# Projection tiles ahead of an attention loop as two 64-row halves side by side

## The chip, the cores and the metric

The kernel runs on one core of a Trainium2 chip. The metric is device time in microseconds (us) of one execution, as the median of several runs. Engines are named as in the profile: PE (TensorE; PEld is its weight load), DVE (VectorE), ACT (ScalarE), POOL (GpSimd), and SP, whose queue issues nearly all DMAs.

## The reference

The input x is 1 x 2048 x 512. After a layer norm without weights, xn goes through attention with 32 heads of 16, and through an MLP that gates the attention's output:

```python
qkv = (xn @ wqkv).reshape(B, S, 3, 32, 16)          # -> q, k, v
p = softmax(einsum("bhqd,bhkd->bhqk", q, k) * 16**-0.5)
s = einsum("bhqk,bhkd->bhqd", p, v) -> (B, S, 512) @ wo
h = relu(xn @ w1 + b1) ** 2                         # 512 -> 1792
g = silu(h @ w2 + b2)                               # 1792 -> 512
out = x + s * g
```

## The kernel before

**Numbers.** All matmuls are fp32r. A product is made from high and low parts of both factors, hi*hi + hi*lo + lo*hi (`terms3`), so a 128 x 512 tile of a projection with a contraction of 512 takes 4 x 3 = 12 matmuls of 128 x 128 by 128 x 512.

**Stages.** First comes the layer norm, with PE transposes and the first projection tiles. Then, ahead of the main loop, 48 rounds of score maxima (`for rnd in range(2 * LEAD)`, L1186). Then the loop of 512 slots, each of which makes exponentials of one block of keys for four heads, P times V, maxima for a later unit, and a share of the MLP. In the loop a slot already runs 64-row matmuls in two lanes: rows 0 to 63 and rows 64 to 127 of the array work on different things at the same time, in different banks.

**A round.** `max_mm(g, j)` for j = 0, 1 (L298 and L305) makes one 64-row matmul of q by k in lane j into a PSUM bank, and DVE reduces the bank to its maxima. Lane 0 uses a bank of pool `pe` (named se, three banks), lane 1 one of pool `pm` (pm_t, three banks). Every third round calls `pump(24)`, which issues 24 matmuls of the projections still to be made: two tiles, one in the bank of pool `pd` (pd_t), one in that of `pv` (po), with all 128 rows (L972 for q and k, L1019 for v). Some rounds also issue loads (`max_end`), the making of a unit's shift (`shift`, L333: four small DVE operations, a store to sh_d and four loads of qe rows from it; here at round 36), the split of the second half of wr_t (round 7) and two splits of w1 (`split_w1`, on POOL, rounds 37 and 41).

**Evacuation of a tile.** A v tile is copied by ACT into a vt buffer and stored (L1025, L1028). A q or k tile is copied by ACT into `raw` (two buffers, L996); POOL makes the high part (L83) and the low part (L84) in `hl` (three buffers); SP stores both parts (L927, `qk_store`). The tiles with m = 0 are split from PSUM by ACT and DVE (`split_psum`, L89 and L90). The last tile, `qk_tile(7, 3, True)`, is left to the first two slots of the loop, which pump six of its matmuls each (L1208), into pd_t.

**Order.** In this stage PE, ACT, DVE and POOL take their instructions in the order of the program. SP's order isn't written out: a planner of the framework lays it from its own estimates, and in the loop SP follows the program too. Every engine works through its queue in order.

Of the kernel before, what the change touches and what calls it, by code (L numbers as in the profile page):

```python
# [9 lines left out]
F32 = mybir.dt.float32  # L10
F32R = mybir.dt.float32r
AF = mybir.ActivationFunctionType
# [5 lines left out]
P = 128  # L18
# [3 lines left out]
DH = 16  # L22
F = 1792
KO = D // P
# [9 lines left out]
NVT = 7  # L34
# [7 lines left out]
def kernel(  # L42
# [11 lines left out]
    nc = tc.nc  # L54
# [24 lines left out]
    def split(dst, raw, hi_act=False, lo=None):  # L79
        if hi_act:  # L80
            nc.scalar.activation(dst[0], raw, AF.Copy)
        else:
            nc.gpsimd.tensor_scalar(dst[0], raw, 1.0, 0.0, op0=ALU.mult, op1=ALU.add)  # L83
        (lo or nc.gpsimd).tensor_tensor(  # L84
            dst[1], raw, dst[0].bitcast(F32), op=ALU.subtract
        )

    def split_psum(hi, lo, ps):
        nc.scalar.activation(hi, ps, AF.Copy)  # L89
        nc.vector.tensor_tensor(lo, ps, hi.bitcast(F32), op=ALU.subtract)  # L90
# [8 lines left out]
    with ExitStack() as ph:  # L99
# [823 lines left out]
        def qk_store(m, c, hl):  # L923
            cs = slice(c * 512, (c + 1) * 512)
            dst = q_d[m] if m < 4 else k_d[m - 4]
            for i in range(2):
                nc.sync.dma_start(dst[i, :, cs], hl[:, i].bitcast(F32))  # L927
# [21 lines left out]
        def when_done(fn):  # L949
            if hold[0]:  # L950
                held.append(fn)
            else:
                fn()

        def let_go():
            while held:
                held.pop(0)()
# [9 lines left out]
        def qk_tile(m, c, last=False):  # L967
            ps = pd.tile([P, 512], F32, name="pd_t") if last else qkv_bank()

            for n0, n1 in ((0, 256), (256, 512)) if c == 0 and m % 4 == 0 else ((0, 512),):  # L970
                for out_, lh, rh, first_, last_ in qk_terms(m, c, ps):
                    nc.tensor.matmul(  # L972
                        out_[:, n0:n1], lh(slice(0, P)), rh(slice(0, P))[:, n0:n1],
                        start=first_, stop=last_,
                    )
                    if not last_ or n1 < 512:
                        yield
            if last:

                hl = pools["n"].tile([P, 2, 512], F32R, name="hl")  # L980
                raw = sp.tile([P, 512], F32, name="ot", bufs=1)
                nc.scalar.activation(raw, ps, AF.Copy)
                split((hl[:, 0], hl[:, 1]), raw)
                later(6, lambda: qk_store(m, c, hl))
                yield
                return

            quick = m % 4 == 0 and not hold[0]

            def evac():  # L990
                hl = hlp.tile([P, 2, 512], F32R, name="hl")
                if quick:
                    split_psum(hl[:, 0], hl[:, 1], ps)
                else:
                    raw = hlp.tile([P, 512], F32, name="raw", bufs=2)
                    nc.scalar.activation(raw, ps, AF.Copy)  # L996
                    split((hl[:, 0], hl[:, 1]), raw)
                qk_store(m, c, hl)

            when_done(evac)  # L1000
            yield

        def qk_first():
            tiles = [qk_tile(m, 0) for m in (4, 0)]
# [3 lines left out]
                        next(tile_)  # L1008
                        yield

        def v_tile(c, tt):
            xT = xTs[c]
            ps = qkv_bank()
            ts_ = slice(tt * P, (tt + 1) * P)
            for out_, lh, rh, first_, last_ in terms3(ps, [
                (lambda a, q, ko=ko: xT[q, a, ko, ts_], lambda b, q, ko=ko: wa_t[q, b, ko, 2 * P :])
                for ko in range(KO)
            ]):
                nc.tensor.matmul(out_, lh(slice(0, P)), rh(slice(0, P)), start=first_, stop=last_)  # L1019
                if not last_:  # L1020
                    yield

            def evac():
                vt = vts[(4 * c + tt) % NVT]
                nc.scalar.activation(  # L1025
                    vt[:, :, :DH], ps.rearrange("p (h d) -> p h d", d=DH), AF.Copy
                )
                nc.sync.dma_start(v_d[:, c * 4 + tt, :], vt.rearrange("p h d -> p (h d)"))  # L1028

            when_done(evac)  # L1030
            yield

        xts = {}

# [41 lines left out]

        ahead = []
        rest = []

        def pump(n):  # L1080
            for _ in range(n):
# [30 lines left out]
        for i in range(NT + 3):  # L1112
            if i in (2, 3):

                kos = slice(2 * i - 4, 2 * i - 2)
                if i == 2:
                    ln_norm(1)
                    ln_high(0)
                    split_w(wa_t, kos, slice(0, 2 * P), raw_m[:, kos])
                else:  # L1120
                    ln_low(0)
                    ln_high(1)
                    split_w(wa_t, kos, slice(0, 2 * P), raw_m[:, kos])
                    ln_norm(2)
                ln_stats(i)
            else:
                if i < NT:
                    ln_stats(i)
                if 0 <= i - 1 < NT:
                    ln_norm(i - 1)  # L1130
                if 0 <= i - 3 < NT:
                    ln_low(i - 3)
                if i == 4:

                    pump(4)
                if 0 <= i - 2 < NT:
                    ln_high(i - 2)
            if 5 <= i < 9:
                split_w(wa_t, i - 5, slice(2 * P, 2 * P + D), raw_v[:, i - 5], True)
            let_go()  # L1140
            if 9 <= i < 11:
                fill_ring("ka", 1, 1.0, (32 + 64 * (i - 9),))
            if i in (11, 12):
                fill_ring("qm", i - 11, 0.0)
            if i == 11:
                raw_r = [load_w("wv", 3 * P, ((P, 3 * P),))]
            if i >= 4:
                pump({4: 4, 7: 14, 8: 12}.get(i, 8 if i < 7 else 7))
            if i == 3:
                ahead.append(qk_first())  # L1150
            if i >= 7 and (i - 3) % 4 == 3:
                c = (i - 3) // 4
                ahead.append(qk_tile(4, c))
                rest.append(qk_tile(0, c))
            if i >= 3 and (i - 3) % 4 == 3:
                c = (i - 3) // 4
                rest += [v_tile(c, tt) for tt in range(4)]
        let_go()
        hold[0] = False
        while ahead:  # L1160
# [12 lines left out]
            fill_ring("qe", n, 0.0)  # L1173
        for n in (2, 3):
            fill_ring("ka", n, 1.0)
        rest += [
            qk_tile(m, c, (m, c) == (7, 3)) for c in range(4) for m in (1, 5, 2, 6, 3, 7)
        ]

        pump(47)  # L1180
        led.append(0)
        pump(24)
        warm = const.tile([P, 1], F32, name="warm")
        nc.scalar.activation(warm, eps_t, AF.Exp)

        for rnd in range(2 * LEAD):  # L1186
            g = rnd // 2
            if rnd % 2 == 0:
                shift_due(g)
            for j in range(2):  # L1190
                max_mm(g, j, None if j else lambda: pe.tile([P, 512], F32, name="se"))
            if rnd % 3 == 2:
                pump(24)
            if rnd % 2 == 0:
                continue
            max_end(g)
            if g == 0:
                raw_r = [load_w("wv", 3 * P, ((D + P, 3 * P),))]
            if g == 3:
                for ko in range(KO):  # L1200
                    split_w(wr_t, ko, slice(3 * P, 6 * P), raw_r[0][:, ko])
                ln.close()
                pools["v"] = ph.enter_context(tc.tile_pool(name="vp", bufs=1))
            if g == 12:
                s1.close()
                ep = ph.enter_context(tc.tile_pool(name="ep", bufs=1))
                rot["pt"] = [ep.tile([P, 512], F32, name=f"pt{i}") for i in range(NPT)]
                pools["n"] = ph.enter_context(tc.tile_pool(name="np", bufs=1))  # L1208
                mlp_early()
            if g in (18, 20):  # L1210
                split_w1((g - 18) // 2)
                load_w1(3 + (g - 18) // 2)
            if g == 16:
                for fo in range(3):
                    load_w1(fo)
                load_v(0)
                nc.sync.dma_start(b1_t, b1.rearrange("(fo p) -> p fo", p=P), allow_slow_non_contiguous=True)
                nc.sync.dma_start(b2_t, b2[None, :].to_broadcast([P, D]))
            if g % 2 and g < 16:
                c, i = divmod(g // 2, 2)  # L1220
                nc.sync.dma_start(
                    xn_d[i, :, :, c * 512 : (c + 1) * 512], xTs[c][:, i].bitcast(F32)
                )
        first.close()

        def exp_mm(st, j, pts, spare):
# [175 lines left out]
        done = 0  # L1402
# [61 lines left out]
```

## Time and profile before

| | |
|---|---|
| median of three runs | 1638.34 us (1637.03 to 1639.03) |
| span of the profiled execution, first to last instruction | 1635.6 us |
| mean granted TensorE clock of it | 0.999 |
| busy: PE, DVE, ACT, POOL | 99%, 83%, 73%, 32% |

The profile is of one execution, and its span leaves out what lies before the first and after the last instruction; the runs' times hold it. A row of the timeline gives start and length in us, engine, line, operation, output and inputs, and in brackets the idle time of the engine before it with what ended it. `64*128 64x512` is a matmul on 64 rows of the array, `128*128 128x512` one on all rows. Matmuls overlap, so their pitch is read from their starts.

### The profile page before, as it was taken

How to read it: one execution, taken by the hardware profiler on the slowest of the kernel's cores; microseconds unless marked ns; L12 is line 12 of the kernel's file. 1: busy time of each engine (PE TensorE's matmuls, PEld its weight loads, DVE VectorE, ACT ScalarE, POOL GpSimd, SP SyncE). 2: the span in 40 equal slices, each digit the busy share in tenths (PEclk: the TensorE clock that was granted, in tenths of full speed). 3: DMA queues.
4: the chain of work that ended last, by engine and by line, in shares of the span. 5: the costliest groups of instructions: out<-in, count | busy, mean ns of one | idle time of the engine just before them, and what ended most of it. 6: DMA issues, size and time to landing. Idle time of an engine off the chain costs nothing.

```text
span 1635.6 us, 35352 instructions
## 1 busy us (share of the span) xinstructions
PE 1620.8 (99%) x13300; PEld 923.2 (56%) x13300; DVE 1356.8 (83%) x2345; ACT 1189.9 (73%) x2351; POOL 523.0 (32%) x547
## 2 busy tenths in 40 slices
PE   8999999999999999999999999999999999999998
PEld 6777565456546655664466456645654565445543
DVE  6356888888888888888888888888888888887754
ACT  7311777777777777877777777777777777777786
POOL 6446568123112311321133112311321233125421
PEclk9999999999999999999999999999999999999999
DMA  8768655434333333434343334323532353246654
GB/s 299 193 210 276 205 171 145 125 100 124 83 95 100 109 93 81 129 87 112 79 121 89 83 90 141 101 68 88 147 98 61 88 144 81 60 130 195 193 170 155
DMA packets 164418, 209.18 MB, mean 128 GB/s; under 512 B 59928, under 2 KB 78872, under 8 KB 162712
## 3 DMA queue, kind: packets, MB, share of 16 engines
q1 hardware_dynamic: 163960, 206.40, 44.5%
q8 instruction: 105, 1.72, 0.5%
q14 instruction: 65, 0.53, 0.1%
q10 hardware_dynamic: 288, 0.52, 0.1%
HBM read 149.95 MB, written 56.61 MB: 126 GB/s over the span
## 4 chain that ended last, share of the span: by engine, by line
PE 99%; DVE 1%; DMA 0%; issue 0%; ACT 0%; POOL 0%; DVEq 0%; POOLq 0%
PE po L373 31%; PE pd_t L242 18%; PE pm_t L298 18%; PE se L1234 15%; PE pd_t L210 6%; PE pd_t L972 2%; PE po L972 2%; PE se L1019 1%; PE se L972 1%; PE pd_t L1019 1%; PE se L298 1%; PE po L1019 1%; PE pm_t L1234 1%; PE pm_t L1065 0%; PE pm_t L811 0%; DVE mx L305 0%
## 5 line engine op out<-in xcount | busy, mean ns | idle before, releaser
L305 DVE TENSOR_REDUCE mx<-pm_t 128x1 f32<-128x512 f32 x2000 | 1245.1, 684 | 167.8 <-PE pm_t L298 77.3
L1246 ACT ACTIVATE pt<-se 128x512 f32<-128x512 f32 x2002 | 1044.2, 617 | 257.6 <-PE se L1234 214.5
L298 PE MATMUL pm_t<-ka,qm 64*128 64x512 f32 x2000 | 793.7, 420 | 1.5 <-DVE mx L305 1.3
L1234 PE MATMUL se<-qe,ka 64*128 64x512 f32 x2002 | 674.0, 396 | 0.2 <-ACT pt L1246 0.2
L373 PE MATMUL po<-pt,v 128*32 128x512 f32 x4096 | 545.3, 604 | 0.0
L298 PEld LDWEIGHTS pm_t<-ka,qm 64*128 64x128 f32 x2000 | 350.1, 184 | 244.8 <-DVE mx L305 230.7
L242 PEld LDWEIGHTS pd_t<-xc,w1s 64*128 64x128 f32 x2688 | 334.0, 187 | 93.9 <-issue 88.9
L242 PE MATMUL pd_t<-xc,w1s 64*128 64x256 f32 x2688 | 380.2, 288 | 0.0
L1234 PEld LDWEIGHTS se<-qe,ka 64*128 64x128 f32 x2002 | 337.6, 184 | 20.7 <-ACT pt L1246 2.6
L242 PE MATMUL pd_t<-w2t,hT 64*128 64x512 f32 x1080 | 300.6, 410 | 0.0
L242 PEld LDWEIGHTS pd_t<-w2t,hT 64*128 64x128 f32 x1080 | 179.1, 184 | 80.5 <-issue 75.5
L529 POOL TENSOR_TENSOR r<-r 128x512 f32<-128x512 f32 x56 | 58.2, 1040 | 374.9 <-ACT r L526 374.9
L373 PEld LDWEIGHTS po<-pt,v 128*32 128x32 f32 x4096 | 81.0, 108 | 158.8 <-issue 136.4
L548 POOL TENSOR_TENSOR u<-u,b_t 128x512 f32<-128x512 f32 x16 | 20.6, 1287 | 316.3 <-ACT u L547 316.3
L411 POOL TENSOR_TENSOR ot<-ot,hl 128x512 f32<-128x512 f32 x31 | 39.8, 1284 | 204.4 <-DMA hl<-r_d 91.1
L210 PE MATMUL pd_t<-wot,oc 64*128 64x512 f32 x336 | 90.9, 406 | 0.0
L526 ACT ACTIVATE r<-pd_t,b_t 128x256 f32<-128x256 f32 x112 | 46.9, 470 | 57.1 <-PE pd_t L242 57.1
L210 PEld LDWEIGHTS pd_t<-wot,oc 64*128 64x128 f32 x336 | 58.4, 184 | 45.4 <-ACT pt L1246 14.2
L84 POOL TENSOR_TENSOR hT<-r,hT 128x512 fp32r<-128x512 f32 x56 | 72.2, 1290 | 4.7
L210 PE MATMUL pd_t<-w2t,hT 64*128 64x512 f32 x264 | 68.8, 393 | 0.0
L305 DVE TENSOR_REDUCE mx<-se 128x1 f32<-128x512 f32 x48 | 32.9, 685 | 40.0 <-PE pm_t L298 30.0
L210 PEld LDWEIGHTS pd_t<-w2t,hT 64*128 64x128 f32 x264 | 47.0, 184 | 6.0
(129 smaller groups left out, 928.5 us busy)
## 6 DMA issues: line engine op xcount, KB each, us to landing
w1s<-w_d SPq DMA_DIRECT2D x196, 256.0 KB
qm<-q_d SPq DMA_DIRECT2D x384, 32.0 KB
ka<-k_d SPq DMA_DIRECT2D x96, 128.0 KB
qe<-q_d SPq DMA_DIRECT2D x384, 32.0 KB
xn_d<-xT SPq DMA_DIRECT2D x8, 1024.0 KB
k_d<-hl SPq DMA_DIRECT2D x32, 256.0 KB
q_d<-hl SPq DMA_DIRECT2D x32, 256.0 KB
xc<-xn_d SPq DMA_DIRECT2D x16, 512.0 KB
```

Of the source, the lines that this page charges most:

```text
L84: (lo or nc.gpsimd).tensor_tensor(dst[1], raw, dst[0].bitcast(F32), op=ALU.subtract)
L210: mm = nc.tensor.matmul(out_, lh(r), rh(r), start=first_ and lane == 0, stop=last_ and lane == 1, skip_group_check=True,)
L242: mm = nc.tensor.matmul(out_, lh(r), rh(r), start=first_ and lane == 0, stop=last_ and lane == 1, skip_group_check=True,)
L298: nc.tensor.matmul(ps, qms[u][p][64 * j : 64 * j + 64, qb * P : (qb + 1) * P], kas[qd, p][64 * j : 64 * j + 64, kc * 512 : (kc + 1) * 512] ...
L305: return nc.vector.tensor_reduce(mxs[u][:, c, kc : kc + 1], ps, axis=AX.X, op=ALU.max)
L373: nc.tensor.matmul(po[32 * j : 32 * j + 32, :], vs[qd][:, (4 * kb + j) * VW : (4 * kb + j) * VW + 32], pts[j], start=(kb == 0), stop=(kb = ...
L526: nc.scalar.activation(r[:, i], ps[:, i * CW : (i + 1) * CW], AF.Relu, bias=b1_t[:, fo : fo + 1])
L529: nc.gpsimd.tensor_tensor(r, r, r, op=ALU.mult)
L972: nc.tensor.matmul(out_[:, n0:n1], lh(slice(0, P)), rh(slice(0, P))[:, n0:n1], start=first_, stop=last_,)
L1019: nc.tensor.matmul(out_, lh(slice(0, P)), rh(slice(0, P)), start=first_, stop=last_)
L1234: nc.tensor.matmul(se, kas[qd, j // 2][b : b + 64, kb * P : (kb + 1) * P], qes[u][j // 2][b : b + 64, :], start=True, stop=True,)
L1246: return nc.scalar.activation(pts[j], se, AF.Exp, scale=0.25)
```

## The change

The 32 tiles that the rounds make are issued by a generator, `side_rounds`, which takes them in groups of four: two in banks of `pm`, two in those of `pd` and `pv`. Each of the 12 matmuls of a tile becomes two of 64 rows. A group has four parts of 12 steps, and a step is one half matmul of one tile in lane 0 and one of another tile in lane 1: tiles 0 and 1; then 2 and 3; then 1 and 0, the lanes crossed; then 3 and 2. After the third part tiles 1 and 0 are evacuated, after the fourth 3 and 2. Every round issues eight steps, so a group takes six rounds and there are eight groups. Both maxima of a round now use banks of `pe`. At the start of a crossed part each lane's first matmul waits, by an added dependency, for the other lane's maximum of a round in between (`since`), so that the two lanes don't write one bank at the same time. The evacuation is moved into functions `qk_done` and `v_done`; tile (m, c) = (0, 3) is now evacuated over `raw` as the others. Ahead of the rounds, the pump stops at the end of tile (0, 2). `qk_tile(7, 3, True)` is left to the slots as before.

```diff
+        def side_tile(kind, a, b, ps):
+
+            if kind == "v":
+                return v_terms(a, b, ps), lambda: v_done(a, b, ps)
+            return qk_terms(a, b, ps), lambda: qk_done(a, b, ps, False)
+
+        def side_rounds(specs):
+
+            assert len(specs) % 4 == 0
+            for n in range(0, len(specs), 4):
+                banks = [pm.tile([P, 512], F32, name="pm_t") for _ in range(2)]
+                tiles = [side_tile(*spec, ps) for spec, ps in zip(specs[n : n + 2], banks)]
+                for part, (a, b) in enumerate(((0, 1), (2, 3), (1, 0), (3, 2))):
+                    if part == 1:
+                        banks = [pd.tile([P, 512], F32, name="pd_t"), pv.tile([P, 512], F32, name="po")]
+                        tiles += [
+                            side_tile(*spec, ps) for spec, ps in zip(specs[n + 2 : n + 4], banks)
+                        ]
+                    for k in range(3 * KO):
+                        for lane, tile_ in enumerate((a, b)):
+                            r = slice(64 * lane, 64 * lane + 64)
+                            out_, lh, rh, first_, last_ = tiles[tile_][0][k]
+                            mm = nc.tensor.matmul(
+                                out_, lh(r), rh(r),
+                                start=first_ and part < 2, stop=last_ and part > 1,
+                                skip_group_check=True,
+                            )
+                            if k == 0 and part > 1:
+                                tc.add_manual_dep(
+                                    mm.ins, since[part][1 - lane].ins.name,
...
+                        yield part, k
+                    if part > 1:
+                        for tile_ in (a, b):
+                            tiles[tile_][1]()
...
-        rest += [
-            qk_tile(m, c, (m, c) == (7, 3)) for c in range(4) for m in (1, 5, 2, 6, 3, 7)
+        rest += [qk_tile(7, 3, True)]
+        later_tiles += [
+            ("qk", m, c) for c in range(4) for m in (1, 5, 2, 6, 3, 7) if (m, c) != (7, 3)
         ]
 
         pump(47)
         led.append(0)
-        pump(24)
+        at = later_tiles.index(("qk", 0, 2)) + 1
+        while len(rest) > 11:
+            pump(1)
+        for _ in rest[0]:
+            pass
+        del rest[: len(rest) - 1]
+        sides = side_rounds(later_tiles[at:])
...
             for j in range(2):
-                max_mm(g, j, None if j else lambda: pe.tile([P, 512], F32, name="se"))
-            if rnd % 3 == 2:
-                pump(24)
+                top = max_mm(g, j, lambda: pe.tile([P, 512], F32, name="se"))
+                since.setdefault(rnd % 6, [None, None])[j] = top
+            for _ in range(8):
+                next(sides, None)
             if rnd % 2 == 0:
                 continue
```

More of the change, by code (lines that the diff above doesn't have):

```diff
@@ L988, in qk_tile, with qk_done @@
             quick = m % 4 == 0 and not hold[0]
[L990 to L1000, printed above, removed]
-            yield
+            when_done(lambda: qk_done(m, c, ps, quick))
+            yield
+        def qk_done(m, c, ps, quick):
+            hl = hlp.tile([P, 2, 512], F32R, name="hl")
+            if quick:
+                split_psum(hl[:, 0], hl[:, 1], ps)
+            else:
+                raw = hlp.tile([P, 512], F32, name="raw", bufs=2)
+                nc.scalar.activation(raw, ps, AF.Copy)
+                split((hl[:, 0], hl[:, 1]), raw)
+            qk_store(m, c, hl)
         def qk_first():
@@ L1009, in qk_first, with v_terms, v_tile @@
                         yield
-        def v_tile(c, tt):
+        def v_terms(c, tt, ps):
             xT = xTs[c]
-            ps = qkv_bank()
             ts_ = slice(tt * P, (tt + 1) * P)
-            for out_, lh, rh, first_, last_ in terms3(ps, [
+            return terms3(ps, [
                 (lambda a, q, ko=ko: xT[q, a, ko, ts_], lambda b, q, ko=ko: wa_t[q, b, ko, 2 * P :])
                 for ko in range(KO)
-            ]):
+            ])
+        def v_tile(c, tt):
+            ps = qkv_bank()
+            for out_, lh, rh, first_, last_ in v_terms(c, tt, ps):
                 nc.tensor.matmul(out_, lh(slice(0, P)), rh(slice(0, P)), start=first_, stop=last_)
@@ L1021, in v_tile, with v_done @@
                     yield
[L1023 to L1030, printed above, removed]
-            yield
+            when_done(lambda: v_done(c, tt, ps))
+            yield
+        def v_done(c, tt, ps):
+            vt = vts[(4 * c + tt) % NVT]
+            nc.scalar.activation(
+                vt[:, :, :DH], ps.rearrange("p (h d) -> p h d", d=DH), AF.Copy
+            )
+            nc.sync.dma_start(v_d[:, c * 4 + tt, :], vt.rearrange("p h d -> p (h d)"))
@@ new lines, in side_tile @@
+        def side_tile(kind, a, b, ps):
[21 more added lines that the diff above has]
+                                skip_group_check=True,
+                            )
+                            if k == 0 and part > 1:
+                                tc.add_manual_dep(
+                                    mm.ins, since[part][1 - lane].ins.name,
+                                    mybir.DependencyInfo(
+                                        mybir.DependencyClass.Sync, mybir.DependencyReason.DATA
+                                    ),
+                                    reason="the other row tile is done with the bank",
+                                )
+                        yield part, k
+                    if part > 1:
+                        for tile_ in (a, b):
+                            tiles[tile_][1]()
@@ L1033 @@
+        since = {}
         xts = {}
@@ L1078 @@
         rest = []
+        later_tiles = []
         def pump(n):
@@ L1154 @@
                 rest.append(qk_tile(0, c))
+                later_tiles.append(("qk", 0, c))
             if i >= 3 and (i - 3) % 4 == 3:
@@ L1157 @@
                 rest += [v_tile(c, tt) for tt in range(4)]
+                later_tiles += [("v", c, tt) for tt in range(4)]
         let_go()
@@ L1223 @@
                 )
+        assert next(sides, None) is None
         first.close()
```

## The prediction

> **What bounds the kernel now.** I read the page first: its first line, the busy shares, and the chain that ended last.
>
> ```profile
> span 1635.6 us, 35352 instructions
> PE 1620.8 (99%) x13300; PEld 923.2 (56%) x13300; DVE 1356.8 (83%) x2345; ACT 1189.9 (73%) x2351; POOL 523.0 (32%) x547
> PE 99%; DVE 1%; DMA 0%; issue 0%; ACT 0%; POOL 0%; DVEq 0%; POOLq 0%
> ```
>
> The matmul queue is never empty for long, and the chain is that queue. So whatever shortens PE's stream in one stage moves the end by as much, unless PE then finds something late. The stage of the change is the 48 rounds of maxima ahead of the loop. The timeline gives its first and its next-to-follow instruction, and the windows view its sums (first PE, then PEld, DVE, ACT, POOL, granted clock, DMA share, GB/s).
>
> ```profile
> 60.54 0.49 PE L298 MATMUL se<-ka,qm 64*128 64x512 f32 x1
> 165.94 0.50 PE L298 MATMUL pm_t<-ka,qm 64*128 64x512 f32 x1
> 60.50:165.90 105.40, 105.40 (x481) 78.68 (x480) 61.74 (x102) 22.28 (x38) 51.66 (x59) 1.00 0.72 238
> ```
>
> The stage takes 165.94 - 60.54 = 105.40 us with PE always busy, DVE at 59%, ACT at 21%, POOL at 49%. One period of three rounds in the timeline:
>
> ```profile
> 107.86 2.99 PE L972 MATMUL pd_t<-xT,wr_t 128*128 128x512 f32 x12
> 110.69 2.88 PE L972 MATMUL po<-xT,wr_t 128*128 128x512 f32 x12
> 113.50 0.50 PE L298 MATMUL se<-ka,qm 64*128 64x512 f32 x1
> 113.84 0.39 PE L298 MATMUL se<-ka,qm 64*128 64x512 f32 x1
> 114.04 0.69 DVE L305 TENSOR_REDUCE mx<-se 128x1 f32<-128x512 f32 x1 [2.87 <-PE pm_t L298]
> 114.07 0.39 PE L298 MATMUL se<-ka,qm 64*128 64x512 f32 x1
> 114.40 0.50 PE L972 MATMUL pd_t<-xT,wr_t 128*128 128x512 f32 x1
> ```
>
> A period is 114.40 - 107.86 = 6.54 us. Inside a run, steps are even: 114.07 - 113.84 = 0.23 for a pair of half-row maxima. At each change of form a step is longer: 0.34 from the first pair (113.50) to the second, 0.33 from the last pair to the first full matmul. 27 even steps of 0.227 would be 6.13; the remaining 0.41 is what two changes of form cost. Sixteen periods: 6.6 us.
>
> **The change part by part.** *Stream in halves.* Each 12-matmul tile becomes 24 half-row matmuls, two tiles side by side: per round 8 pairs and one pair of maxima, 9 x 48 = 432 pairs, no change of form. No row shows two projection halves running together in this stage; the nearest are the loop's blocks, where one half accumulates and the other overwrites, and the tail, where both accumulate (L796):
>
> ```profile
> 305.42 0.39 PE L1234 MATMUL se<-qe,ka 64*128 64x512 f32 x1
> 306.79 0.40 PE L1234 MATMUL se<-qe,ka 64*128 64x512 f32 x1
> 307.29 0.39 PE L1234 MATMUL se<-qe,ka 64*128 64x512 f32 x1
> 1625.91 0.39 PE L796 MATMUL pm_t<-wot,q 64*128 64x512 f32 x1
> 1626.14 0.39 PE L796 MATMUL pd_t<-w,q 64*128 64x512 f32 x1
> ```
>
> Six pairs take 1.37 us (0.228 each), all eight 1.87 (0.234, the last two slowed), the tail's 0.23. I take 0.231: 432 x 0.231 = 99.8, and 0.1 for the one change of form at the start. The next stage could start at 60.54 + 99.9 = 160.4 instead of 165.94: **gain 5.5** (ends: 6.6 at 0.2285, 4.2 at 0.234). A round is then 2.08 us.
>
> *Maxima.* DVE has two reductions per 2.08 us at a pitch of 0.6. The pair's second is done 0.54 + 0.6 + 0.69 = 1.83 us after the pair starts. The new wait of a crossing half (it needs the other lane's last maximum of the round before) comes at 2.08 + 0.23 = 2.31: 0.5 us spare, so nothing. If it were late, everything behind it on PE would stand, sixteen times over.
>
> *Evacuation* now comes as two tiles together every three rounds, in four banks: ACT copy, two POOL operations, two stores. Its rows, and those of the work that POOL and SP do in between:
>
> ```profile
> 107.14 0.60 ACT L996 ACTIVATE raw<-po 128x512 f32<-128x512 f32 x1 [2.12 <-POOL hl L84]
> 107.83 0.63 POOL L83 TENSOR_SCALAR hl<-raw 128x512 fp32r<-128x512 f32 x1 [0.73 <-ACT raw L996]
> 108.54 1.28 POOL L84 TENSOR_TENSOR hl<-raw,hl 128x512 fp32r<-128x512 f32 x1
> 157.40 0.41 POOL L83 TENSOR_SCALAR w1s<-ex 128x256 fp32r<-128x256 f32 x1
> 159.08 0.73 POOL L84 TENSOR_TENSOR w1s<-ex,w1s 128x256 fp32r<-128x256 f32 x1
> 134.90 0.20 DVE L335 STREAM_TRANSPOSE tr<-m 128x32 f32<-128x32 f32 x1
> 136.20 0.19 DVE L338 SCALAR_TENSOR_TENSOR sh<-tr,sh 128x32 fp32r<-128x32 f32 x1
> 144.15 0.38 SPq L344 DMA_DIRECT2D sh_d<-sh  x1
> 144.63 0.85 SPq L927 DMA_DIRECT2D k_d<-hl  x2
> 147.57 2.24 SPq L364 DMA_DIRECT2D qe<-sh_d  x4
> 148.99 0.62 POOL L83 TENSOR_SCALAR hl<-raw 128x512 fp32r<-128x512 f32 x1 [2.09 <-DMA k_d<-hl]
> 149.85 0.42 SPq L927 DMA_DIRECT2D q_d<-hl  x1
> 152.37 0.62 POOL L83 TENSOR_SCALAR hl<-raw 128x512 fp32r<-128x512 f32 x1 [1.38 <-DMA q_d<-hl]
> ```
>
> A tile costs POOL 2.0 us (L83 to the end of L84), so two take 4.0 of 6.2 us: enough on the average. But a copy needs one of two raw buffers, freed only by POOL, and a tile one of three hl buffers, freed only by landed stores: 2.5 us after issue (149.85 to 152.37) at best, up to 3.9 (second store of 144.63, issued near 145.1, to 148.99). Two places get tight.
>
> First place, round 36. In the built order of the changed kernel SP has the store of the shift (sh_d) and the four reads of it ahead of the stores of the first two tiles of group 5 (rounds 30 to 35, groups counted from 0), which are ready from round 34.5. The shift itself is made at round 36; in the trace of before SP did this at leisure. Counted from the start of round 36: DVE takes 136.39 - 134.90 = 1.5 us and starts 0.2 early (1.83 of 2.08), 1.3; sh_d lands, 2.5 like the quick store, 3.8; four reads issued, 6.0; first tile's second store issued 0.42 later and landed 2.5 after that, 9.0. Only then has POOL a buffer for group 5's fourth tile: done 11.0; then split_w1 in POOL's order (157.40 to 159.81, 2.4): 13.4; group 6's first two tiles: 17.4; then raw is free and ACT can empty group 6's pd bank: 18.0. PE wants that bank at round 43.5, 7.5 x 2.08 = 15.6. **PE waits 2.4** (none if the stores landed at once; 3.4 and a wait of 1.0 at round 42 if sh_d takes the 3.4 of 144.15 to 147.57 and the stores 3.6).
>
> Second place, the loop's start. The rows:
>
> ```profile
> 166.12 0.60 ACT L996 ACTIVATE raw<-po 128x512 f32<-128x512 f32 x1 [2.12 <-POOL hl L84]
> 166.60 1.65 PE L972 MATMUL pd_t<-xT,wr_t 128*128 128x512 f32 x6
> 166.62 1.08 ACT L1246 ACTIVATE pt<-se 128x512 f32<-128x512 f32 x2
> 168.18 0.50 PE L298 MATMUL pm_t<-ka,qm 64*128 64x512 f32 x1
> ```
>
> Slot 0 needs pd for qk_tile(7,3) 0.66 us after it starts (166.60); the bank was long free. Now it holds a tile that ends with the rounds (T). Its copy is behind a raw buffer that POOL frees after two tiles: T - 3.12 + 0.27 + 0.60 + 0.07 + 4.0 = T + 1.8, and 0.65 more for the copy: T + 2.5, against T + 0.56 (no change of form before it): **PE waits 2.0**, and the exponentials stand behind that copy on ACT. The later maxima come after those six matmuls, so it isn't regained.
>
> Also, around round 20 SP's queue has both b_t loads ahead of three tiles' stores:
>
> ```profile
> 138.71 3.32 SPq L1217 DMA_DIRECT2D b_t<-in_B_b_dram  x1
> 142.07 1.99 SPq L1218 DMA_DIRECT2D b_t<-in_B_b_dram  x1
> ```
>
> That is 5.3 us, with large xn_d stores just ahead in the queue. The same chain of buffers then reaches PE at round 25.5: between 0 and 2.5 us. I take 0.3, near the lower end, since the bank becomes free within 0.2 us of being wanted when stores land in 2.5.
>
> *Nothing* for v tiles (ACT alone), for the second half of wr_t (split at round 7, wanted at round 13.5) and for the quick copy of qk_tile(0,3) moved from DVE to POOL (DVE has room).
>
> Sum: -5.5 + 2.4 + 2.0 + 0.3 = -0.8. The span goes from 1635.6 to 1634.8. The median of the runs, 1638.34, stands 2.7 above that span, so the prediction is 1637.5.
>
> **The rivals.** *Neither store chain binds.* If stores land early enough, round 43.5 has no wait; then -5.5 + 2.0 = -3.5, 1634.8, and 1632.8 without the wait in slot 0. For it: in the waits view of before, POOL waited for stores only three times in this stage. Against: those three come right behind the sh_d store.
>
> ```profile
> POOL hl L83 <- DMA k_d<-hl: 3.2, 2, 2.1
> POOL hl L83 <- DMA q_d<-hl: 1.4, 1, 1.4
> ```
>
> *Slower: the stores land late.* Decided by landing time: at 3.6 instead of 2.5 us, sh_d at 3.4 and the b_t block 2 us later, the waits are 2.5 (round 25.5), 1.0 and 3.4 (rounds 42 and 43.5) and 2.1, together 9.0: +3.5, 1641.8. For it: rows with 3.4 and 3.9, and DMA at 0.72 of the stage. Against: SP stands still before the chain at round 36, so its transfers meet little traffic.
>
> *Slower: halves aren't free.* If each pair cost more than the loop's, PE would pay 432 times. The slowed end of the block is (307.29 - 306.79) / 2 = 0.25; 432 x 0.25 = 108.0, +2.7 instead of -5.5. Rounds of 2.25 shrink the wait at round 43.5 to 18.0 - 16.9 = 1.1 and that in slot 0 to 1.8: +5.6, 1643.9. It decides from a pair of about 0.241 on. Against: the even steps of 0.228 and the tail's 0.23. The Trainium skill, TensorEngine Tiling (Array Packing), section Performance Considerations, states about 60 cycles of overhead for each matmul, and recommends row tiling for contractions of 64 or less, not for splitting one of 128; by that rule twice the matmuls would be a loss. At the 2.4 GHz of its page TensorE: Matmul & The Clock Gate (table of specifications) that is an estimate of 25 ns, a pair of 0.252. The even steps of this trace show no such addition.
>
> **How the numbers follow.** From no change I can tell about 0.2%, 3.3 us: 1635.1 to 1641.6. The forecast has 0.50, all of it within. No store chain: 0.22, faster. Late stores: 0.18, half of it beyond the bound. Dear halves: 0.10, slower. With a little of the forecast's own tail on the slow side: faster 0.22, same 0.55, slower 0.23. The range leaves out dear halves (0.10) and the outer end of the first rival (some 0.08): 1633.5 to 1642.5.
>
> **What would show it.** In the changed trace: the rounds as pairs at 0.23 with PE starting round 43 or so about 90 us after round 0; a gap before a pd_t half there, released by ACT raw; POOL waiting for q_d<-hl some 4 to 5 us after round 36; L972's first matmul 2.5 us after slot 0 starts. Wrong would be even pairs over 0.24, no gap at round 43.5, or waits on DVE at the crossings.

## The result and the profile after

Over 18 runs each, the changed kernel takes 1640.25 us in the median (1639.18 to 1641.62) and the kernel before 1637.66 (1636.67 to 1639.04): ratio 1.0015 [1.0009, 1.0021], so 2.6 us slower, and outside what the measurement leaves to chance. The profiled spans say the same: 1638.5 against 1635.6, 2.9 more. The page of the changed kernel, its first line, the busy shares and the chain by engine:

```profile
span 1638.5 us, 36113 instructions
PE 1617.9 (99%) x13684; PEld 944.5 (58%) x13684; DVE 1357.2 (83%) x2344; ACT 1188.4 (73%) x2351; POOL 524.7 (32%) x549
PE 94%; ACT 2%; DMA 1%; DVE 1%; SPq 1%; POOL 1%; issue 0%; POOLq 0%; DVEq 0%; ACTq 0%
```

PE's busy time fell by 2.9 us although the span grew by 2.9, and PE's share of the chain fell from 99% to 94%: the chain now leaves PE and runs through ACT, POOL, SP and DMA. Where it does so, the timeline of PE shows. These are the first matmul of the rounds, the two places where PE stands, and the first matmul of slot 0:

```profile
60.60 0.50 PE L298 MATMUL se<-ka,qm 64*128 64x512 f32 x2
118.04 0.79 PE L1057 MATMUL pd_t<-xT,wr_t 64*128 64x512 f32 x1 [4.06 <-ACT raw L998]
167.07 0.39 PE L298 MATMUL pm_t<-ka,qm 64*128 64x512 f32 x1
169.67 1.65 PE L972 MATMUL pd_t<-xT,wr_t 128*128 128x512 f32 x6 [1.91 <-ACT raw L998]
```

The stage from round 0 to slot 0 takes 167.07 - 60.60 = 106.47 us, against 105.40 before. 45 of its 48 rounds run close to the forecast of 2.08: 2.07 to 2.10 us each at first (2.19 the very first, which holds the change of form), and 2.06 from round 15 on, a pair of halves every 0.229. Rounds 25, 26 and 27 start at 112.59, 119.92 and 123.76, and round 28 at 125.88: 13.29 us for three rounds that should take 6.18. These 7.11 us are the whole loss of the stage; without them it would take 99.36 us, a gain of 6.04. They have two parts, which the windows view tells apart (first PE, then PEld, DVE, ACT, POOL, granted clock, DMA share, GB/s):

```profile
113.00:118.00 5.00, 0.98 (x9) 0.55 (x6) 1.29 (x2) 0.60 (x1) 2.46 (x3) 0.91 1.01 258
118.00:121.00 3.00, 2.96 (x14) 2.37 (x16) 0.42 (x1) 0.00 (x0) 1.28 (x1) 0.50 0.90 233
121.00:124.00 3.00, 3.00 (x16) 2.31 (x16) 0.87 (x2) 0.00 (x0) 1.47 (x2) 0.52 1.03 374
124.00:130.00 6.00, 6.00 (x55) 5.70 (x55) 3.87 (x6) 1.09 (x2) 2.36 (x4) 1.00 0.40 152
```

PE stands for 4.06 us. When it goes on, the granted clock is 0.50 for nearly six microseconds and a pair takes about 0.425 instead of 0.229; that is nearly all of the other 3.05 us. The Trainium skill, TensorE: Matmul & The Clock Gate, Part 1, states that a window of about 3.4 us of idleness puts the array on half its clock until it has been busy for as long. The rows agree on the half clock (0.50 after 4.06 us of idleness); it lasted longer, nearly six microseconds after PE had gone on.

Why PE stood is in the chain of waits of the changed kernel, followed back from that matmul (start, length, piece; the small "issue" pieces are left out):

```profile
90.25 1.25 SPq L1276
...
92.88 10.78 DMA xn_d<-xT
103.68 0.35 SPq L1273
104.13 0.38 SPq L927
...
105.07 4.18 DMA v_d<-vt
...
109.30 0.40 SPq L438
...
109.80 0.45 SPq L927
...
110.34 4.88 DMA q_d<-hl
...
115.40 0.63 POOL hl L83
116.10 1.27 POOL hl L84
117.39 0.61 ACT raw L998
118.04 0.79 PE pd_t L1057
```

Read downwards: SP issues 1 MB stores of xn_d and then other loads; the second bias load (L1273) has to wait until one of these stores has landed, 10.78 us after its issue, and SP stands 1.4 us for it; behind it leave the first q_d stores; the load at L438 waits until a v_d store has landed (4.18 us after its issue; SP stands 1.7); only then leave the stores of the tile whose hl buffer POOL wants, and they take 4.88 to land. POOL makes its two halves, a raw buffer is free, ACT copies, and PE has its bank. The waits view of 58 to 175 us has POOL standing for these stores three times, 13.5 us in all, where before it was 1.4 and 3.2 (columns: us in total, times, longest):

```profile
POOL hl L83 <- DMA q_d<-hl: 13.5, 3, 5.7
```

There is no third place in the rounds or at the start of slot 0. At round 43.5, where the prediction had its largest wait, PE does not stand at all. The timeline shows why:

```profile
137.81 0.20 DVE L335 STREAM_TRANSPOSE tr<-m 128x32 f32<-128x32 f32 x1
138.48 0.32 SPq L344 DMA_DIRECT2D sh_d<-sh  x1
139.98 2.25 SPq L364 DMA_DIRECT2D qe<-sh_d  x4
142.33 0.86 SPq L927 DMA_DIRECT2D q_d<-hl  x2
```

Round 34 starts at 138.24. The shift is made there, not at round 36 as the prediction and the description of the kernel above have it; the trace of before had said so too, for DVE's row at 134.90 stands between the maxima of round 33 (from 133.70) and those of round 34 (from 136.31). And sh_d had landed 1.5 us after its issue, where the prediction took 2.5.

### The profile page after: what moved, and what is told of

It is laid out like the page before. It is cut to its first block, busy times and chain, and to the rows that moved or that the text cites. A ratio compares the mean times of both kernels' runs of the same rounds, so it can differ in the third digit from the quotient of the medians.

```text
span 1638.5 us, 36113 instructions
## 1 busy us (share of the span) xinstructions
PE 1617.9 (99%) x13684; PEld 944.5 (58%) x13684; DVE 1357.2 (83%) x2344; ACT 1188.4 (73%) x2351; POOL 524.7 (32%) x549
## 4 chain that ended last, share of the span: by engine, by line
PE 94%; ACT 2%; DMA 1%; DVE 1%; SPq 1%; POOL 1%; issue 0%; POOLq 0%; DVEq 0%; ACTq 0%
PE po L373 30%; PE pd_t L242 19%; PE pm_t L298 17%; PE se L1290 14%; PE pd_t L210 6%; ACT pt L1302 2%; PE pm_t L1057 2%; PE se L1021 1%; PE pd_t L1057 1%; PE se L972 1%; PE po L1057 1%; DMA xn_d<-xT 1%; PE se L298 0%; PE pm_t L1109 0%; PE pm_t L811 0%; POOL hl L84 0%
## 5 line engine op out<-in xcount | busy, mean ns | idle before, releaser
L305 DVE TENSOR_REDUCE mx<-pm_t 128x1 f32<-128x512 f32 x1952 | 1212.5, 684 | 167.5 <-PE pm_t L298 79.0
L298 PE MATMUL pm_t<-ka,qm 64*128 64x512 f32 x1952 | 778.7, 420 | 1.5 <-DVE mx L305 1.3
L298 PEld LDWEIGHTS pm_t<-ka,qm 64*128 64x128 f32 x1952 | 343.0, 184 | 243.2 <-DVE mx L305 230.3
L305 DVE TENSOR_REDUCE mx<-se 128x1 f32<-128x512 f32 x96 | 61.8, 686 | 42.1 <-PE se L298 42.1
```

What stands on the lines that cost most here:

```text
L298: nc.tensor.matmul(ps, qms[u][p][64 * j : 64 * j + 64, qb * P : (qb + 1) * P], kas[qd, p][64 * j : 64 * j + 64, kc * 512 : (kc + 1) * 512] ...
L305: return nc.vector.tensor_reduce(mxs[u][:, c, kc : kc + 1], ps, axis=AX.X, op=ALU.max)
```

## The experiments

Ratios are against the kernel before, whose median was 1637.7 to 1638.0 in these comparisons. "Stage" is the time from round 0 to slot 0 in the profiled execution (105.40 before; 99.36 with no wait in the rounds), "pump" the time from the start of slot 0 to its first full matmul (0.66 before; 2.60 in the changed kernel).

| kernel | median us | ratio [95%] | stage | pump |
|---|---|---|---|---|
| changed kernel | 1640.25 | 1.0015 [1.0009, 1.0021] | 106.47 | 2.60 |
| four raw buffers | 1632.73 | 0.9968 [0.9957, 0.998] | 99.36 | 1.42 |
| three raw buffers | 1634.18 | 0.9977 [0.9968, 0.9987] | 100.57 | 1.41 |
| four hl buffers | 1635.54 | 0.9988 [0.9979, 0.9998] | 100.37 | 2.60 |
| PE kept busy at round 25.5 | 1639.07 | 1.0008 [0.9999, 1.0017] | 103.50 | 2.60 |
| bias loads later | 1639.64 | 1.0011 [1.0002, 1.0021] | 105.94 | 2.61 |
| other order of two evacuations | 1641.69 | 1.0024 [1.0014, 1.0033] | 108.16 | 1.13 |
| SP in program order | 1647.75 | 1.0059 [1.0045, 1.0072] | 111.34 | 2.61 |
| the same, four raw buffers | 1642.35 | 1.0027 [1.0017, 1.0036] | 101.80 | 3.32 |
| before, four raw buffers | 1637.74 | 0.9999 [0.999, 1.0009] | 105.40 | 0.67 |
| before, 48 changes of form | 1651.62 | 1.0085 [1.0071, 1.0099] | 118.67 | 0.66 |

The theory to be tested: the rounds are worth their 6 us, and two waits for a bank that ACT hasn't emptied, one of them with a slow clock behind it, take more than that back. The rival: the gain does not last, whatever is done to the waits.

### Four raw buffers

```diff
-                raw = hlp.tile([P, 512], F32, name="raw", bufs=2)
+                raw = hlp.tile([P, 512], F32, name="raw", bufs=4)
```

> The changed kernel with four raw buffers for ACT's copies instead of two; every engine's order, SP's included, is unchanged. Theory A (two waits for an evacuated bank cost the change its gain): ACT no longer needs POOL to be done before it copies a bank, so the wait of PE at round 25.5 (4.1 us, with the slow pairs after it 7.1) and the one in slot 0 (1.9) both go: 1640.3 - 9 = 1631.3 us, 6.4 below before. Theory B (the halves' gain doesn't last, a later stage takes it back): the rounds end 7 us earlier, but the loop then waits for loads or splits of w1, and the time stays within 2 us of before, 1635.7 to 1639.7.

Measured: 1632.73, span 1630.1, 8.4 below the changed kernel. Slot 0 and its first full matmul in the timeline:

```profile
60.40 0.50 PE L298 MATMUL se<-ka,qm 64*128 64x512 f32 x2
159.76 0.39 PE L298 MATMUL pm_t<-ka,qm 64*128 64x512 f32 x1
161.18 1.63 PE L972 MATMUL pd_t<-xT,wr_t 128*128 128x512 f32 x6 [0.73 <-ACT raw L998]
```

All rounds are even; POOL is as late as before, but no longer in PE's way:

```profile
111.10 0.59 ACT L998 ACTIVATE raw<-pd_t 128x512 f32<-128x512 f32 x1
115.28 0.62 POOL L83 TENSOR_SCALAR hl<-raw 128x512 fp32r<-128x512 f32 x1 [4.65 <-DMA q_d<-hl]
```

The copy that ended at 118.0 in the changed kernel is done at 111.7, while POOL's wait for the store is the same 4.65. The theory holds and the rival falls: the gain lasts to the end. 1.4 us are missing from the expected 1631.3, of which the wait left in slot 0 explains 0.7. This version beats both kernels by more than the measurement is uncertain.

### The kernel before with four raw buffers

The same edit at its L995.

> The kernel before with four raw buffers instead of two, the order of every engine as it was. Theory A (PE of before waits for no bank in this stage, so the buffers are worth something only to the changed order of projections): 1637.7, within 0.05% of before. Rival (the buffers are a gain of their own, which the changed kernel with four of them merely showed): 1633 to 1635, ratio at most 0.998; then the halves are worth much less than the 6 us that I put down to them.

1637.74, nothing. The stage has the same 105.40 and PE is busy throughout (windows view):

```profile
60.50:165.90 105.40, 105.40 (x481) 78.64 (x481) 61.62 (x102) 22.29 (x38) 51.39 (x59) 1.00 0.71 235
```

The 5 us that the version with four raw buffers gains on the kernel before are therefore the halves' work; the buffers only let it through.

### What a change of form costs

The kernel before, with its projections spread over all rounds:

```diff
-            if rnd % 3 == 2:
-                pump(24)
+            pump(8)
```

> The kernel before, with the projections spread finer: 8 full matmuls after each of the 48 rounds of maxima instead of 24 after every third, so 48 changes from half rows to full rows and back instead of 16. If the gain of the changed rounds is the price of these changes (0.41 us for a pair of changes, read from one period of before), 32 more pairs cost 32 x 0.41 = 13.1 us: 1637.7 + 13.1 = 1650.8, ratio 1.008 (between 1.006 and 1.010), and the rounds take 118.5 us instead of 105.4. If the 0.41 were a cost of the first maxima after a long run, or of DVE's turn, and not of the change of form, the time stays within 3 us of 1637.7.

1651.62, 13.9 more. The stage runs from the first of these rows to the second:

```profile
62.93 0.49 PE L298 MATMUL se<-ka,qm 64*128 64x512 f32 x1
181.60 0.50 PE L298 MATMUL pm_t<-ka,qm 64*128 64x512 f32 x1
```

118.67 - 105.40 = 13.27 us for 32 more pairs of changes: 0.415 each, against 0.41 from one period of before. So the source of the gain is what the prediction said.

### PE kept busy at round 25.5

36 useless half matmuls into two se banks, ahead of group 4's second part; their results are not used.

```diff
+                    if n == 16 and part == 1:
+                        fill = [pe.tile([P, 512], F32, name="se") for _ in range(2)]
+                        for _ in range(18):
+                            for lane in range(2):
...
```

> The changed kernel with 18 pairs of half-row matmuls of no use (into two free se banks, never read) at the place of the wait at round 25.5, so that PE works through the 4.1 us instead of standing still. Theory A1 (the slow pairs of 0.43 us after the wait come from PE's idleness, which lowers its granted clock): the pairs after it stay at 0.23, the 2.9 us that the slow ones cost are saved, 1637.4 us. Theory A2 (the slow pairs come from the heavy DMA traffic in that stretch, 0.9 and more of its share): they stay slow, 1640.3 us or up to 1641 where the useless pairs outlast the wait.

The windows view of the same stretch as above:

```profile
113.00:118.00 5.00, 5.00 (x46) 4.94 (x45) 1.29 (x2) 0.60 (x1) 2.33 (x3) 1.00 1.02 291
118.00:121.00 3.00, 3.00 (x29) 3.00 (x28) 1.29 (x2) 0.00 (x0) 1.50 (x2) 1.00 0.97 235
```

The clock stays at 1.00 under the same DMA load, and pairs stay at 0.23. The stage is 103.50: 4.14 above 99.36, the length of the filling, and the 3.0 us of slow pairs are gone. So those came from PE's idleness and not from the transfers. The median of 1639.07 is only 1.2 below the changed kernel, and the span 2.4; the stage is the sharper reading. Over the eleven runs the mean granted clock lay between 0.997 and 1.000 (0.999 in the profiled one), so in some of them the clock still fell.

### The order of two evacuations

```diff
-                        for tile_ in (a, b):
+                        for tile_ in (b, a):
```

This also moved some of SP's planned instructions.

> The changed kernel with the two tiles of each evacuation in the other order, pd_t ahead of po. SP's planned order changes a little with it: the store of tile (1, 0) comes ahead of the second b_t load. Theory A: pd_t is copied at once when the rounds end, so the wait in slot 0 goes (1.9 us). At round 25.5 it is then po that is copied last, and PE wants both banks there, so that wait stays unless SP's store, one load earlier, shortens it by up to 2: 1636.5 to 1638.4 us. Theory B: nothing gained, 1640.

```profile
121.91 0.79 PE L1057 MATMUL po<-xT,wr_t 64*128 64x512 f32 x1 [6.77 <-ACT raw L998]
170.91 1.65 PE L972 MATMUL pd_t<-xT,wr_t 128*128 128x512 f32 x6 [0.31 <-ACT raw L998]
```

The wait in slot 0 went from 1.91 to 0.31, since pd's tile is now copied first: that part of the theory holds. But the wait at round 25.5 grew from 4.06 to 6.77, as SP's stores left later still (the one that POOL waited for at 115.4 instead of 110.3), and the total was 3 us above what I expected. I had not asked what the edit does to the planned queue.

### SP in program order

```diff
+        by_hand = first.enter_context(tc.manual_schedule(engines={mybir.EngineType.SP}))
```

> The changed kernel with SP's queue in program order during the rounds instead of the planner's order: xn_d's 1 MB stores are spread over the rounds, and the b_t loads come behind the ones of w1 and v at round 33. Theory A: the stores of tile (1, 0) no longer stand behind four 1 MB stores and two b_t loads, POOL gets its hl buffer in time, and the wait at round 25.5 with its slow pairs goes (7.1 us); the wait in slot 0 stays: 1633.2 us. Rival A3 (two raw and three hl buffers are too few for pairs of tiles whatever SP's order): a wait of 1 to 4 us shows up at another round, 1635 to 1641 us.

A miss on the slow side, and the most telling run. Round 25 has no wait at all. Round 43 has one:

```profile
160.79 0.79 PE L1057 MATMUL pd_t<-xT,wr_t 64*128 64x512 f32 x1 [9.12 <-ACT raw L998]
```

The chain of this kernel behind it:

```profile
142.47 0.69 DVE mx L305 x2
143.16 2.97 DMA sh_d<-sh
146.15 0.62 SPq L364
...
148.95 2.80 DMA q_d<-hl
...
151.93 0.62 POOL hl L83
```

In program order the bias loads come in round 33 and the shift's store and reads right behind them, ahead of group 5's stores. That is the prediction's first place, sh_d ahead of those stores with POOL starved of hl buffers and PE standing at round 43.5, with 9.1 us instead of 2.4. The larger wait comes with the loads ahead of it in SP's queue: round 34 starts at 131.74, but sh_d leaves only at 143.16, behind the loads of w1, v and the biases. So the mechanism exists; in the changed kernel's own order the stall does not occur. Both orders have one place where SP's queue holds the stores of two tiles for too long.

With four raw buffers as well:

> The changed kernel with SP in program order through the rounds, and four raw buffers. With two, the round at 25.5 had no wait, but round 43 took 12.4 us and round 44 3.7 (9.1 us of waiting for a bank, then pairs at 0.42 us), since SP stands at the b_t loads and the store of the shift ahead of group 5's stores, and slot 0 had its 2 us. Theory A (all of these are waits for an evacuated bank, which two more raw buffers outlast): rounds all 2.06, 12.0 less there and 1.2 in slot 0, 1647.75 - 13.2 = 1634.5, and no clock below 0.9 in the rounds. Rival (POOL itself is late by 12 us for want of hl buffers, so four raw buffers only put the wait off to slot 0, where PE waits 5 us or more): 1638 to 1642.

1642.35, 8 above the theory's figure and just beyond the rival's. Round 43 and slot 0 keep waits:

```profile
154.13 0.50 PE L1057 MATMUL pd_t<-xT,wr_t 64*128 64x512 f32 x1 [2.08 <-ACT raw L998]
166.72 2.85 PE L972 MATMUL pd_t<-xT,wr_t 128*128 128x512 f32 x6 [2.70 <-ACT raw L998]
```

Two more raw buffers do not outlast this delay: the rest is put off into slot 0, as the rival said. The span of the profiled execution is 3.3 us above before (1638.9 against 1635.6). Stage and pump explain 0.3 us of it net (-3.6 and +2.7, and 1.2 for the slowed matmuls of the last row); the rounds start 1.1 later (61.60 against 60.54), PE waits 1.4 for a read of xn_d in the loop, and 0.5 is left unexplained. The median of the runs is another 1.7 above the profiled run, which no trace shows.

### Three raw buffers, or four hl buffers

The same lines with `bufs=3`, and `right(qs, "hlp", 4)` instead of 3.

> The changed kernel with three raw buffers instead of two. Theory A: at round 25.5 the copy that PE waits for finds the third buffer free and starts when its bank is full, near 114 us in place of 117.4, so rounds 25 to 27 are 2.06 each (7.1 less, 2.9 of it the slow clock); in slot 0 the copy waits for one tile on POOL instead of two, 2.0 less: 1640.25 - 7.1 - 1.9 = 1631.3 to 1633, as with four. Rival (one buffer only defers the chain by one tile of POOL, 2 us, so 2 us of wait stay at round 25.5, too short to slow the clock): about 1635 to 1636.

> The changed kernel with four hl buffers instead of three and two raw buffers as it was (as much memory as four raw buffers), the order of every engine unchanged. Theory A (PE waits because POOL stands for an hl buffer whose store hasn't landed): with a fourth, the two pm_t tiles of round 24 go through POOL at about 108.5 to 112.4 us, the raw buffer is free for pd_t's copy before 114, so rounds 25 to 27 are 2.06 each, 7.1 less; the 1.9 us in slot 0 stay, since there the copy waits for POOL's four microseconds and not for a store: 1640.25 - 7.1 = 1633.1. Rival (the stores land so late that a fourth buffer is full as soon): 3 us or more of wait stay at round 25.5 or come at round 31.5: 1636 to 1640.

Three raw buffers: 1634.18. Round 25.5 is free of waits, slot 0 as with four; but a new wait of 0.84 comes one group later, and round 31 is 1.2 longer. Four hl buffers: 1635.54, with 0.63 of wait at round 31.5 and the whole wait in slot 0 as expected:

```profile
126.23 0.50 PE L1057 MATMUL pd_t<-xT,wr_t 64*128 64x512 f32 x1 [0.63 <-ACT raw L998]
162.84 2.54 PE L972 MATMUL pd_t<-xT,wr_t 128*128 128x512 f32 x6 [1.97 <-ACT raw L998]
```

Both totals lie between the theory's figure and the rival's. Either buffer removes the 7.1 us at round 25.5, and so each of the links, raw or hl, was necessary for that wait. What I left out both times is that the delay then passes to the next group. For the same memory, two raw buffers bring 2.8 us more than one hl buffer, as they act on both places.

### The bias loads behind the rounds

```diff
-                nc.sync.dma_start(b1_t, b1.rearrange("(fo p) -> p fo", p=P), allow_slow_non_contiguous=True)
-                nc.sync.dma_start(b2_t, b2[None, :].to_broadcast([P, D]))
...
         assert next(sides, None) is None
+        nc.sync.dma_start(b1_t, b1.rearrange("(fo p) -> p fo", p=P), allow_slow_non_contiguous=True)
+        nc.sync.dma_start(b2_t, b2[None, :].to_broadcast([P, D]))
```

> The changed kernel with the two loads of the biases (b_t) asked for behind the rounds instead of in round 33; only SP's order changes. In the trace of the changed kernel they stand on SP from 101.85 to 104.1 us, the second until the last xn_d store has landed, ahead of the stores of the tile that holds the buffer. Theory A (these loads are what holds the stores, as the prediction named them): the stores leave about 2.2 us earlier, PE's wait at round 25.5 falls from 4.1 to about 1.9 us, which is too short to slow the clock: 1640.25 - 5.1 = 1635.1. Rival (the xn_d stores in the same queue hold whatever stands behind them until 103.7): at most 0.8 us earlier, a wait of 3.3 us or more: 1637 to 1640.

```profile
103.96 0.81 SPq L927 DMA_DIRECT2D q_d<-hl  x2
...
115.70 0.49 PE L1057 MATMUL pd_t<-xT,wr_t 64*128 64x512 f32 x1 [1.53 <-ACT raw L998]
...
131.29 0.79 PE L1057 MATMUL pd_t<-xT,wr_t 64*128 64x512 f32 x1 [2.92 <-ACT raw L998]
```

The wait at round 25.5 fell to 1.53, about as the theory said, and the clock did not drop there. But the first stores left at 103.96, hardly earlier than 104.13: as the rival said, SP stood behind xn_d all the same, and the gain at this place came from L438, which still stands between the two tiles' stores but waits 0.6 us for v_d instead of 1.7 (109.80 became 108.60 for the second tile's stores, and POOL had its buffer at 113.04 instead of 115.40). And round 31.5 now has a wait of 2.92 and slow pairs behind it, since SP stood in reads of qe and in the two loads at their new place, again ahead of stores. Total 1639.64, within the rival's range. Moving one load in a planned queue moved the stall and did not remove it.

## Why the prediction was wrong

It was 1637.5 with a gain of 0.8 over before; the change cost 2.6. By its steps:

- **Rounds, -5.5.** Right, and a little small: 99.36 us for 432 pairs is 0.230 each, and the gain is 6.04. The price of a change of form (0.41) was measured as 0.415.
- **Crossings, 0.** Right: no wait on DVE at any of the sixteen.
- **Slot 0, +2.0.** Right: 1.94 (2.60 against 0.66), at the named place, by the named copy.
- **Round 43.5, +2.4.** Wrong: 0. The shift's round was misread, 36 for 34, and two rounds are 4.1 us of slack. The mechanism itself was right, as SP in program order showed.
- **Round 25.5, +0.3 out of 0 to 2.5.** This is the step that failed. Place and chain were right, the size was 7.11: 4.06 of waiting and 3.05 of slow clock.

-6.04 + 7.11 + 0 + 1.94 = 3.0, against 2.9 between the two spans. That the forecast of the span, 1634.8, missed 1638.5 by no more than 3.7 is in part luck: 6.8 too little at round 25.5 stands against 2.4 too much at round 43.5 and 0.5 too little gain in the rounds. Of the rivals, the dear halves fall, since they needed pairs of 0.241 or more.

Two things made the failed term so small. I took 2.5 us for a store to land and costed the bias loads by themselves, though I named the xn_d stores ahead of them. In the crowded queue xn_d took 10.78, v_d 4.18 and q_d 4.88, and SP stood for the first two in turn (1.4 and 1.7 us). The rival "stores land late" was the right idea but spread its price over four places, with 2.5 here. Second, no term had a price for what a wait does to the matmuls behind it. The Trainium skill, TensorE: Matmul & The Clock Gate, Part 1, has that price, half the rate after idleness, and the prediction had taken only the page's full clock from it; the measured amount is the 3.05 us above.

## What to carry to other kernels

When a change makes PE denser, price the chain that empties its banks in the busiest place of the DMA queue, not in a quiet one: count every transfer that the issuing queue may stand behind, each with its landing time there. Price also what a longer wait of PE does to the matmuls behind it: in these rounds waits of 2.92, 6.77, 9.12 and 4.06 us cost 1.8, 2.0, 2.9 and 3.05 us beyond their own length, since those matmuls ran on half the clock. Where such a chain nearly reached PE, more buffers were worth more here (7.5 us for two raw buffers, 4.7 for one hl buffer) than moving single transfers (0.6 at best), which shifted the stall.

## What was not expected of the hardware

**The clock falls after less idleness than the 3.4 us that the Trainium skill states (TensorE: Matmul & The Clock Gate, Part 1).** After 1.53 us (bias loads later), 1.84 (PE kept busy, slot 0), 1.91 (changed kernel, slot 0) and 2.08 (SP in program order with four raw buffers, round 43.5) it stayed. After 1.97 it stayed in one kernel (bias loads later, slot 0) and fell in two, one of which is the kernel with four hl buffers: the six matmuls of its last row take 2.54 instead of 1.65. After 2.70, 2.92, 4.06 and more it fell each time. The windows of that kernel and of the one with later bias loads:

```profile
162.00:163.00 1.00, 0.16 (x1) 0.16 (x2) 0.00 (x0) 0.81 (x2) 0.92 (x3) 1.00 0.47 176
163.00:164.00 1.00, 1.00 (x4) 0.75 (x5) 0.00 (x0) 0.77 (x2) 1.00 (x1) 0.66 1.05 375
164.00:165.00 1.00, 1.00 (x4) 0.56 (x2) 0.00 (x0) 0.00 (x0) 0.92 (x3) 0.50 0.43 162
166.00:167.00 1.00, 1.00 (x8) 0.35 (x4) 0.86 (x2) 0.83 (x2) 0.05 (x1) 0.64 0.46 172
```

```profile
130.00:132.00 2.00, 0.71 (x4) 0.61 (x6) 0.00 (x0) 0.60 (x1) 1.92 (x3) 0.76 0.75 277
132.00:133.00 1.00, 1.00 (x8) 0.81 (x6) 0.00 (x0) 0.00 (x0) 1.00 (x2) 0.50 0.96 344
```

What decides between 1.9 and 2.1 us is where the wait lies. In each trace the changes of the clock lie 3.41 us apart, or a whole multiple of it. With four hl buffers the clock falls at 163.32 and rises at 166.73 (the means of 0.66 and 0.64 above), in the changed kernel at 117.06 and 123.89; with SP in program order it changes at 155.96, 166.20, 176.44 and 183.27. The falls at 163.32 and 176.44 come 0.5 and 1.3 us after PE has gone on, so no wait set them off by its length alone. Continue each trace's steps of 3.41 us, and the waits sort themselves. The two of 1.97 with a fall lie each within one step. The one of 1.97 without is cut into 1.2 and 0.8, that of 2.08 into 1.1 and 0.9, that of 1.91 into 0.5 and 1.4. So in these traces the clock fell at the end of a step in which PE was idle for 1.97 us or more, and stayed when it was 1.53 or less; between the two no wait lies.

**Half rows side by side cost next to nothing.** Two 64-row matmuls, together a full one's work, keep a pitch of 0.229 to 0.230 against 0.227 of full matmuls, over 432 pairs.
